# Loading C by heads from two queues at the start of a fused state-space and hardswish kernel

## Chip, cores and metric

The kernel runs on one core of one Trainium2 chip. The metric is the device time of one execution in microseconds; where several executions were timed, their median is given with the lowest and the highest.

A core has a matrix engine (PE, with its weight loads listed apart as PEld), a vector engine (DVE), a scalar engine (ACT), GpSimd (POOL) and a synchronisation engine (SP). Each has its own instruction stream and works through it in order; they wait for each other on semaphores. In this kernel DMA loads and stores are issued by SP and, for two loads at the start, by ACT.

## The reference, cut to what is computed

```python
batch, n_heads, seq, head_dim, d_state = (4, 8, 768, 32, 16)
...
for c in range(nc):                       # chunks of tokens
    cum = np.cumsum(la, axis=-1)          # la: log of the clipped a
    L = np.exp(cum[:, :, :, None] - cum[:, :, None, :]) * causal
    CB = np.einsum('bhin,bhjn->bhij', Cc, Bc)
    y_intra = np.einsum('bhij,bhjd->bhid', CB * L, xc)
    y_inter = np.einsum('bhin,bhnd->bhid', Cc, state) * np.exp(cum)[:, :, :, None]
    y[:, :, sl] = y_intra + y_inter
    Bx = np.einsum('bhjn,bhjd->bhjnd', Bc, xc) * decay_from_j[:, :, :, None, None]
    state = decay_full[:, :, None, None] * state + np.sum(Bx, axis=2)
...
x = y.transpose(0, 2, 1, 3).reshape(3072, 256)
h = x @ w_in                              # w_in: 256 x 2048
g = h * np.clip(h + 3.0, 0.0, 6.0) / 6.0
out = g @ w_out                           # w_out: 2048 x 256
```

x, a, B and C come as 32-bit floats. The two weight matrices come as 64-bit floats, which the kernel decodes into 32-bit floats itself.

## The kernel before, in words

**Tiling.** The sequence of 768 tokens is cut into six chunks of 128. A chunk has all four batches and eight heads; within a chunk the decays are kept for two halves of 64 tokens. For each chunk the state-space part gives `yT` (256 model columns by 512 tokens), and the two matrix products follow: `h`, sixteen tiles of 128 columns, and the output. Later chunks use a scheme of seven products with sums of weights in place of eight; the first chunk (0) doesn't. The loop over chunks overlaps the products of one chunk with the state-space part of the next.

**The order is written out by hand.** Tiles take their semaphores from the program, but each engine carries its instructions out in the order of the source. The opening, lines 938 to 985, is a list of calls that sets up chunk 0: everything there must be done before the first `mlp_in` (L616) can start. DMA loads take one of eight semaphores in turn, so a load that comes round to a semaphore waits, on its issuing engine, for the load that had it before.

**Names that matter.**

- `load_bc(0)` (L85) loads C and B of chunk 0. C goes through `pairs_first` (L96): eight loads on SP, one for each batch and each parity of head, of 32 KB in pieces of 256 bytes. The result `pairs` has in its partitions four pairs of heads by 32 groups of four tokens. B goes through `tokens_first` (L91): one load of 256 KB in pieces of 64 bytes, for chunk 0 on ACT's queue.
- `load_w(0)` (L142) brings the first quarter of `w_in`, 1 MB of 64-bit numbers, on ACT's queue, ahead of B. `load_x(0)` and `load_w(1)` follow on SP; `load_w(2)` and `load_w(3)` stand further down in the opening.
- `decode(i)` (L187) is a generator that turns a quarter of weights into 32-bit floats. Each `weights(i, n)` carries it on by n steps. For quarter 0 the steps are: (1) ACT copies the top words, `ws` (L198), and DVE makes the significands in two steps (L201, L205); (2) DVE picks exponent bits and sign (L215, L217); (3) ACT turns exponents into a scale (L221); (4) again on ACT (L223); (5) DVE joins them (L228, L236) into `w_in`.
- `log_a`, `add_up`, `in_three`: the logarithms, the running sums (a DVE scan, L269, in two parts) and their split into three parts, from which PE builds differences in PSUM (`diff`, L348 and L357).
- `diff_exp(c, b)` (L365): ACT takes the exponential of a difference bank. For chunk 1, batches 2 and 3, these banks are the same ones that the first chunk's state products (L539) and outputs write to.
- `first_eto` (L376): the decay from the start of the chunk.
- `turn_squares` (L465): DVE transposes `pairs` in squares of 32; `part_heads` (L472): two copies by parity of the head. Together they give C as `cT` and `csT`. `turn_b` (L431): PE transposes B (L422), ACT copies it to `bT`.
- `ends(0, b)` (L396): POOL scales B by the decays, `bs`. `fade` (L478): POOL scales half of `csT`.
- `scores(0)` (L527, L539): PE makes C times B, `cb`, and then the state products from x and `bs`. `multiply(0)`: ACT copies `adds` and `mid`, DVE multiplies the decays by `cb` (L568).
- `turn_cum` (`c_ps`, L316), `busy` (L490, two matmuls whose result nobody reads), `mix` (L594, L500), `keep` (ACT's four copies to `yT`, L608).
- `store_rows` (L286, L288) stores the running sums to DRAM, from where later chunks read their decays.

Of the kernel before, what the change touches and what calls it, by code (L numbers as in the profile page):

```python
# [8 lines left out]
FP32 = mybir.dt.float32  # L9
# [11 lines left out]
def kernel(  # L21
# [24 lines left out]
    nc = tc.nc  # L46
    P = 128
    NB, NH, S, D = x.shape
    N = B.shape[-1]
# [14 lines left out]
    loads = ctx.enter_context(tc.tile_pool(name="loads", bufs=2))  # L64
# [17 lines left out]
    Bs, bcs, xts = {}, {}, {}  # L82
    TURN = 3

    def load_bc(c):  # L85

        sl = slice(c * P, (c + 1) * P)

        def tokens_first(src, queue=nc.sync, **where):  # L91
            t = loads.tile([P, NB * NH, N], FP32, **where)
            queue.dma_start(out=t, in_=src[:, :, sl, :].rearrange("b h s n -> s (b h) n"))
            return t

        def pairs_first(src):  # L96
            t = loads.tile([P, 2, NB, 4, N], FP32, name="pairs", tag="bc")
            for b in range(NB):
                for h in range(2):
                    nc.sync.dma_start(  # L100
                        out=t[:, h, b].rearrange("s a n -> s (a n)"),
                        in_=src[b, h:NH:2, sl, :].rearrange("h (s a) n -> h s (a n)", a=4))
            return t

        if 0 < c < TURN:
            bcs[c] = [tokens_first(C, name="C", tag="bc")]
        Bs[c] = tokens_first(B, nc.scalar if c == 0 else nc.sync, name="B")
        if c == 0:
            bcs[c] = [pairs_first(C), Bs[c]]
        elif c < TURN:  # L110
            bcs[c].append(Bs[c])
        else:
            bcs[c] = [pairs_first(C), pairs_first(B)]
# [14 lines left out]
    def load_w(i, queue=nc.sync):  # L128

        raw = loads.tile([P, NK * FP * 2 * P], U32, name="raw", bufs=NRAW)  # L130
        if i < NP:
            cols = slice(2 * i * FP * P, 2 * (i + 1) * FP * P)
            src = moe_w_in[:, cols].rearrange("(k p) f -> p k f", p=P)
            dst = raw.rearrange("p (k f) -> p k f", k=NK)
        else:
            r0 = (i - NP) * FP * P
            src = moe_w_out[r0:r0 + FP * P, :].rearrange("(k p) m -> p k m", p=P)
            dst = raw.rearrange("p (k m) -> p k m", k=FP)
        queue.dma_start(out=dst, in_=src)
        raws[i] = raw  # L140

    load_w(0, nc.scalar)  # L142
    load_bc(0)
    load_x(0)
    load_w(1)
# [9 lines left out]
    def conceal_in(t, pattern):  # L155
# [24 lines left out]
        out=head, in_=head, pattern=[[-2 * N, NQ], [-N, 2]], compare_op=ALU.is_ge,  # L180
        fill=0.0, base=0, channel_multiplier=1)
    nc.gpsimd.affine_select(
        out=head, in_=head, pattern=[[2 * N, NQ], [N, 2]], compare_op=ALU.is_ge,
# [66 lines left out]
    ends_at = (slice(0, 2 * P), slice(2 * P, S))  # L250
# [17 lines left out]
    def add_up(sl):  # L268
        nc.vector.tensor_tensor_scan(  # L269
            out=cum[:, sl], data0=run.rearrange("g c p -> g (c p)")[:, sl], data1=a_sb[:, sl],  # L270
            initial=0.0, op0=ALU.mult, op1=ALU.add)
# [13 lines left out]
    def store_rows():  # L285
        nc.sync.dma_start(  # L286
            out=cum_e[1:].rearrange("c g p -> g c p"), in_=cum_c[:, 1:])
        nc.sync.dma_start(  # L288
            out=cum_d[2:].rearrange("c a g i -> g (c a) i"),
            in_=cum[:, 2 * P:].rearrange("g (k i) -> g k i", i=HT))  # L290
# [71 lines left out]
    def diff_exp(c, b):  # L362
        if c not in Ls:
            new_decays(c)
        nc.scalar.activation(Ls[c][:, b], ds.pop((c, b)), AF.Exp)  # L365

    def first_eto():

        e_ps = ps.tile([P, NB, HT], FP32, name="e_ps", tag="f0")
        for b in range(NB):  # L370
            nc.tensor.matmul(
                out=e_ps[:, b],
                lhsT=picks[:, b * P:(b + 1) * P],
                rhs=split[:, 0, HALF[1]], start=(b == 0), stop=True, skip_group_check=True)
        etos[0] = att.tile([P, NB, P], FP32, name="eto")
        nc.scalar.activation(etos[0][:, :, HALF[1]], e_ps, AF.Exp)  # L376
# [14 lines left out]
    def ends(c, b):  # L391

        if b == 0:
            bss[c] = att.tile([P, G, N], FP32, name="bs")
        hs = slice(b * NH, b * NH + NH)
        nc.gpsimd.tensor_tensor(  # L396
            out=bss[c][:, hs], in0=Bs[c][:, hs],
            in1=Ls[c][:, b, :, HT - 1:HT].to_broadcast([P, NH, N]), op=ALU.mult)
# [8 lines left out]
    def turned(c):  # L407
        if c not in bTs:
            bTs[c] = [att.tile([P, NB, P], FP32, name="bT", bufs=1),
                      att.tile([P, NB, 2, P], FP32, name="cT", bufs=1),  # L410
                      att.tile([P, NB, P], FP32, name="csT", bufs=1)]
        return bTs[c]

    def turn_ps(c, j):

        if c < 2:
            return ps.tile([P, NB, P], FP32, name="t_ps", tag=f"f{2 * j if c else 1}")
        return ps_o.tile([P, NB, P], FP32, name="t_ps", tag="o")

    def transposes(c, j, t_ps):  # L420
        for b in range(NB):
            nc.tensor.transpose(  # L422
                out=t_ps[:, b],
                in_=bcs[c][j][:, b * NH:(b + 1) * NH].rearrange("s h n -> s (h n)"),
                identity=ident)

    def turn_b(c):

        t_ps = turn_ps(c, 1)
        transposes(c, 1, t_ps)  # L430
        nc.scalar.copy(out=turned(c)[0], in_=t_ps)  # L431
# [31 lines left out]
    def turn_squares(t, out):  # L463

        nc.vector.transpose(  # L465
            out=out.rearrange("r b (s a) -> r b a s", a=4),
            in_=t.rearrange("s t b a n -> s (b a) t n"))

    def part_heads(c):
        _, cT, csT = turned(c)  # L470
        for t in range(2):
            nc.vector.tensor_scalar(  # L472
                out=cT[:, :, t], in0=csT, scalar1=parity[:, t:t + 1], scalar2=None,
                op0=ALU.mult)

    def fade(c, sl=slice(0, P), engine=nc.vector):
        csT = turned(c)[2][:, :, sl]
        engine.tensor_tensor(out=csT, in0=csT, in1=etos[c][:, :, sl], op=ALU.mult)  # L478
# [443 lines left out]
    def load(c):  # L922
        load_bc(c)
        load_x(c)
# [3 lines left out]
    def weights(i, n):  # L928
        for _ in range(n):
            next(parts[i], None)  # L930


    def diff(c, *bs):
        for part in (diff_less, diff_pick):
            for b in bs:
                part(c, b)
# [10 lines left out]
        mask_again(0, b)  # L947
    diff(0, 0, 1)
    diff(0, 2, 3)
    weights(0, 1)  # L950
    for b in range(NB):
        diff_exp(0, b)
    first_eto()
    diff(1, 2, 3)
    weights(0, 1)
    for b in range(NB):
        ends(0, b)
    turn_b(0)
    diff(1, 0, 1)
    weights(0, 1)  # L960
    diff_exp(1, 2)
    diff_exp(1, 3)
    turn_squares(bcs[0][0], turned(0)[2])
    part_heads(0)
    fade(0, HALF[1], nc.gpsimd)
    add_up(ends_at[1])
    store_rows()
    load_w(2)
    weights(0, 1)
    scores(0)  # L970
# [22 lines left out]
    for k in range(NC):  # L993
        gTs[k] = ffn.tile([P, NF, TB], FP32, name="gT")
        c, ahead = k + 1, k + 2
# [70 lines left out]
        for i, _ in enumerate((wide_units if c < NC else out_units)(k)):  # L1066
            if i == 0:
                s = NJ - 1
# [58 lines left out]
```

## Time and profile before

| What | Value |
|---|---|
| median of 3 runs | 355.81 us (355.05 to 355.95) |
| the profiled execution's own time | 355.29 us |
| its span, first to last instruction | 353.6 us |
| PE busy | 343.7 us, 97% of the span |
| DVE busy | 227.4 us, 64% |
| ACT busy | 178.7 us, 51% |
| POOL busy | 138.0 us, 39% |
| granted PE clock | 1.000 |
| read from HBM, written | 21.07 MB, 3.29 MB |

The profile is of one execution. The span leaves out 1.7 us that lie around the instructions. Times inside it are in microseconds from its start. Busy time of PE is the time in which a matmul is under way, so a high share means that PE is seldom without one. A row of the timeline gives start, length, engine, source line, operation, what is written and read, and in brackets how long the engine stood idle before and what ended that. The chain of waits is found backwards from the last instruction: at each step it goes to what released it.

The opening, in windows (us from the start, then busy time of each engine with the number of instructions, granted clock, DMA share, GB/s):

```profile
0.00:7.40 7.40, 4.42 (x10) 1.38 (x10) 4.46 (x17) 3.13 (x5) 2.75 (x13) 1.00 0.84 189
7.40:13.00 5.60, 5.35 (x144) 3.37 (x144) 2.73 (x6) 3.82 (x8) 1.52 (x4) 1.00 0.82 113
13.00:22.76 9.76, 6.58 (x294) 5.00 (x295) 9.34 (x15) 5.68 (x11) 1.50 (x1) 1.00 0.99 303
```

The engines stand in the order PE, PEld, DVE, ACT, POOL.

### The profile page before, as it was taken

The numbers are of one execution on the slowest core, as the hardware profiler recorded it, in microseconds if no ns is written. First come the engines' busy times: TensorE is split into PE (matmuls) and PEld (weight loads), VectorE is DVE, ScalarE is ACT, GpSimd is POOL, SyncE is SP. The second block draws the span as 40 slices with busy tenths as digits, with TensorE's granted clock in tenths as the row PEclk, the third lists the DMA queues.
The fourth block names the chain that finished last, engine by engine and source line by source line (L and its number), as shares of the span: only waits on it lengthen the run. The fifth ranks groups of instructions, "written<-read, shape, count | busy, mean of one in ns | idle before, by whom it ended". The sixth has DMA issues, their size and how long they took to land.

```text
span 353.6 us, 8557 instructions
## 1 busy us (share of the span) xinstructions
PE 343.7 (97%) x3488; PEld 281.9 (80%) x3488; DVE 227.4 (64%) x426; ACT 178.7 (51%) x394; POOL 138.0 (39%) x139
## 2 busy tenths in 40 slices
PE   6699999999999999999999999999999999999996
PEld 2454458888887888888888888888888888888996
DVE  6689999975797437786437787436687322688111
ACT  4768887258764741665641575551575011466100
POOL 3300000362498621099612099710078600068700
PEclk9999999999999999999999999999999999999999
DMA  8999969502925052256034256001200001200000
GB/s 168 178 335 162 272 157 122 128 2 78 164 55 66 4 125 51 35 70 81 2 72 97 36 67 91 4 4 18 34 9 1 4 3 20 34 8 2 0 32 30
DMA packets 91607, 24.92 MB, mean 70 GB/s; under 512 B 84208, under 2 KB 87952, under 8 KB 91056
## 3 DMA queue, kind: packets, MB, share of 16 engines
q1 hardware_dynamic: 87184, 23.06, 35.7%
q10 hardware_dynamic: 4384, 1.31, 1.7%
q8 instruction: 27, 0.44, 0.5%
q14 instruction: 12, 0.10, 0.1%
HBM read 21.07 MB, written 3.29 MB: 69 GB/s over the span
## 4 chain that ended last, share of the span: by engine, by line
PE 91%; DVE 3%; DMA 3%; ACT 1%; SPq 1%; issue 1%; DVEq 0%; ACTq 0%
PE even L658 18%; PE odd L658 13%; PE wb L836 12%; PE wc L836 8%; PE o L713 8%; PE h L616 8%; PE wa L836 8%; PE oa L772 4%; PE ob L772 4%; PE y L594 3%; PE y L500 2%; PE cb L527 2%; DMA raw<-in_moe_w_in_dram 2%; PE y L539 1%; DMA pairs<-in_C_dram 1%; SPq L100 1%
## 5 line engine op out<-in xcount | busy, mean ns | idle before, releaser
L758 POOL TENSOR_TENSOR s<-gT 128x512 f32<-128x512 f32 x20 | 26.3, 1317 | 86.0 <-DVE gT L699 86.0
L658 PE MATMUL even<-ts,w_sum 128*128 128x256 f32 x160 | 48.2, 383 | 0.0
L694 ACT ACTIVATE gT<-odd,half 128x512 f32<-128x512 f32 x40 | 27.5, 688 | 34.9 <-DVE odd L687 34.9
L658 PE MATMUL odd<-yT,w_in 128*128 128x256 f32 x160 | 41.1, 379 | 0.0
L673 ACT COPY even<-odd 128x512 f32<-128x512 f32 x40 | 23.0, 576 | 27.7 <-PE odd L658 25.5
L658 PEld LDWEIGHTS even<-ts,w_sum 128*128 128x128 f32 x160 | 29.9, 190 | 5.3 <-ACT up L680 1.5
L699 DVE SCALAR_TENSOR_TENSOR gT<-gT,odd 128x512 f32<-128x512 f32 x40 | 27.5, 688 | 9.9 <-ACT gT L694 9.9
L658 PEld LDWEIGHTS odd<-yT,w_in 128*128 128x128 f32 x160 | 30.4, 190 | 4.1
L385 ACT ACTIVATE L<-L,cum_n 128x64 f32<-128x64 f32 x128 | 31.5, 340 | 0.0
L836 PE MATMUL wb<-s,w_out 128*128 128x256 f32 x128 | 30.7, 382 | 0.0
L694 ACT ACTIVATE gT<-even,half 128x512 f32<-128x512 f32 x40 | 27.8, 695 | 4.4 <-PE even L658 4.4
L699 DVE SCALAR_TENSOR_TENSOR gT<-gT,even 128x512 f32<-128x512 f32 x40 | 27.2, 679 | 4.4 <-ACT gT L694 4.4
L713 PE MATMUL o<-w_out,gT 128*128 128x256 f32 x128 | 28.7, 381 | 0.0
L616 PE MATMUL h<-yT,w_in 128*128 128x512 f32 x64 | 27.7, 594 | 0.0
L674 DVE COPY up<-odd 128x256 f32<-128x256 f32 x40 | 16.9, 423 | 15.8 <-ACT even L673 15.1
L713 PEld LDWEIGHTS o<-w_out,gT 128*128 128x128 f32 x128 | 24.1, 190 | 3.7 <-issue 0.5
L403 POOL TENSOR_TENSOR tmp<-state,eto 128x256 f32<-128x256 f32 x5 | 3.4, 684 | 60.4 <-DMA eto<-cum_e 51.1
L836 PEld LDWEIGHTS wb<-s,w_out 128*128 128x128 f32 x128 | 24.0, 190 | 3.4
L758 POOL TENSOR_TENSOR s<-s,gT 128x512 f32<-128x512 f32 x20 | 25.5, 1273 | 1.6
L758 POOL TENSOR_TENSOR gT<-gT 128x512 f32<-128x512 f32 x20 | 25.4, 1272 | 0.0
L758 POOL TENSOR_TENSOR s<-gT,s 128x512 f32<-128x512 f32 x20 | 25.4, 1270 | 0.0
L658 PE MATMUL even<-yT,w_sum 128*128 128x256 f32 x80 | 24.4, 387 | 0.2
(150 smaller groups left out, 657.9 us busy)
## 6 DMA issues: line engine op xcount, KB each, us to landing
raw<-in_moe_w_out_dram SPq DMA_DIRECT2D x4, 1024.0 KB
L<-cum_d SPq DMA_DIRECT2D x8, 512.0 KB
xt<-in_x_dram SPq DMA_DIRECT2D x6, 512.0 KB
raw<-in_moe_w_in_dram SPq DMA_DIRECT2D x3, 1024.0 KB
out_dram<-back SPq DMA_DIRECT2D x128, 16.0 KB
eto<-cum_e SPq DMA_DIRECT2D x20, 64.0 KB
B<-in_B_dram SPq DMA_DIRECT2D x5, 256.0 KB
raw<-in_moe_w_in_dram ACTq DMA_DIRECT2D x1, 1024.0 KB
```

The lines of the kernel that those rows point to most:

```text
L385: nc.scalar.activation(Ls[c][:, b, h], Ls[c][:, b, h], AF.Exp, bias=cum_n[:, c, g:g + 1])
L594: nc.tensor.matmul(out=ys[c][a, u][d0:d0 + D, b], lhsT=xt[rows, b * NH + h], rhs=Ls[c][rows, b, h], start=(b == 0 and a >= min(c, 1)), sto ...
L616: nc.tensor.matmul(out=h.rearrange("p r i -> p (r i)"), lhsT=w_in[:, j, f * P:(f + 1) * P], rhs=yTs[k][:, j].rearrange("p b i -> p (b i)") ...
L658: nc.tensor.matmul(out=bank[:, r], lhsT=lhsT, rhs=rhs, start=start, stop=True, skip_group_check=True)
L673: nc.scalar.copy(out=even, in_=odd[:, 1:2].to_broadcast([P, 2, 2 * P]))
L674: nc.vector.tensor_copy(out=up[:, 1], in_=odd[:, 0])
L694: nc.scalar.activation(gTs[k][:, f], h.rearrange("p r i -> p (r i)"), AF.Relu, bias=half, scale=1.0 / 6.0)
L699: nc.vector.scalar_tensor_tensor(out=g, in0=g, scalar=1.0, in1=h.rearrange("p r i -> p (r i)"), op0=ALU.min, op1=ALU.mult)
L713: nc.tensor.matmul(out=o[:, b % 2], lhsT=gTs[0][:, f, b * P:(b + 1) * P], rhs=w_out[:, f], start=(f == 0 and b % 2 == 0), stop=True, skip_ ...
L758: nc.gpsimd.tensor_tensor(out=o, in0=p_, in1=q_, op=op)
L772: nc.tensor.matmul(out=bank[:, slot], lhsT=lhs[:, j], rhs=rhs[:, j], start=(clear and j == 0), stop=True, skip_group_check=True)
L836: nc.tensor.matmul(out=bank[:, slot], lhsT=lhs[:, j], rhs=rhs[:, j], start=(clear and j == 0), stop=True, skip_group_check=True)
```

## The change

Four things change, all in the opening.

1. C of chunk 0 is loaded by `heads_first`: eight loads, one for each head, each into 32 partitions with all four batches. The size and the pieces of 256 bytes are those of before, and so is the layout of the result. The first three go out on ACT's queue, the other five on SP's. `load_w(0)` stands on ACT's queue behind those three.
2. B of chunk 0 goes out on SP's queue behind C, ahead of x.
3. `turn_squares` and `part_heads` move up, from behind the exponentials of chunk 1 to directly behind the difference matmuls, ahead of the first step of decoding.
4. The first step of decoding moves down behind `diff_exp(0, b)` and `first_eto`; the second behind `turn_b`. The second scan and `store_rows` move up ahead of it.

```diff
+        def heads_first(src, between):
+            t = loads.tile([P, 2, NB, 4, N], FP32, name="pairs", tag="bc")
+            for i in range(NH):
+                if i == 3:
+                    between()
+                (nc.scalar if i < 3 else nc.sync).dma_start(
+                    out=t[32 * (i // 2):32 * (i // 2) + 32, i % 2].rearrange("s b a n -> s b (a n)"),
+                    in_=src[:, i, sl, :].rearrange("b (s a) n -> s b (a n)", a=4))
+            return t
...
-        Bs[c] = tokens_first(B, nc.scalar if c == 0 else nc.sync, name="B")
         if c == 0:
-            bcs[c] = [pairs_first(C), Bs[c]]
+            bcs[c] = [heads_first(C, lambda: load_w(0, nc.scalar))]
+        Bs[c] = tokens_first(B, name="B")
+        if c == 0:
+            bcs[c].append(Bs[c])
...
-    load_w(0, nc.scalar)
     load_bc(0)
...
     diff(0, 2, 3)
-    weights(0, 1)
+    turn_squares(bcs[0][0], turned(0)[2])
+    part_heads(0)
     for b in range(NB):
         diff_exp(0, b)
     first_eto()
+    weights(0, 1)
     diff(1, 2, 3)
-    weights(0, 1)
+    add_up(ends_at[1])
+    store_rows()
     for b in range(NB):
         ends(0, b)
     turn_b(0)
+    weights(0, 1)
     diff(1, 0, 1)
     weights(0, 1)
     diff_exp(1, 2)
     diff_exp(1, 3)
-    turn_squares(bcs[0][0], turned(0)[2])
-    part_heads(0)
     fade(0, HALF[1], nc.gpsimd)
-    add_up(ends_at[1])
-    store_rows()
     load_w(2)
```

## The prediction

> **What bounds the kernel now.** I read the busy table first: TensorE (PE) is busy 97% of the span. The slices place the idle rest: of the 40 only the first two and the last show 6 tenths, all others 9 or more, and a table of windows says it finely: PE is busy 16.36 of the first 22.76 us, 27.74 of the 27.74 up to 50.50, and 299.64 of the 303.10 behind that. So the opening is what can be won, and whatever moves PE's first `h` matmul (22.76) moves the end by as much. The chain of waits in order of time (start us, length us, what), for the opening:
>
> ```profile
> 0.80 5.81 DMA raw<-in_moe_w_in_dram
> ...
> 6.63 0.67 SPq L100
> ...
> 7.34 1.47 SPq L100
> ...
> 8.86 3.94 DMA pairs<-in_C_dram
> ...
> 12.97 1.10 DVE csT L465
> ...
> 14.10 0.89 DVE cT L472 x2
> ...
> 15.13 1.25 PE cb L527 x60
> ...
> 16.38 1.30 DVE L L568 x2
> ...
> 17.72 0.43 PE c_ps L316 x4
> 18.15 1.05 PE d L490 x2
> ```
>
> C is late. SP's sixth C load waits until the first weights (w0) have landed (6.62), since it reuses their semaphore; the last leaves at 8.86 and lands at 12.79. Then transpose, parity copies, scores, product, and PE's mixing until `h`. C is slow too, by the DMA totals of two windows (4 to 5.5 us, then 8 to 10 us; columns: packets, MB, packets' time as a share of 16 engines):
>
> ```profile
> q10 hardware_dynamic: 212, 0.59, 100.8%
> ```
> ```profile
> q10 hardware_dynamic: 479, 0.03, 18.6%
> q1 hardware_dynamic: 266, 0.07, 18.3%
> ```
>
> q10 is ACT's queue (w0, then B), q1 is SP's (a, C, x, w1). While w0 flows no C packet moves, though four C loads are out; later C moves 0.07 MB in 2 us with the DMA engines a third busy.
>
> **The change, part by part.**
>
> *C by heads[...].* In that window 266 C packets of 256 B take 18.3% x 16 x 2 us, 22 ns each. [...] All of C, 1024 packets, is then an estimate of [...]64 x 22 ns = 1.4 us by the row spread over 16 engines[...]. I take 1.4: the window in which x flows has more packets per engine than C needs, and only the last two pieces (0.35 us, or 0.7) stand on the path.
>
> *Order of issue.* ACT now issues three C pieces, then w0. At 0.49 us each (its B issue), w0 leaves at 2.27, not 0.80, and the table load ends at 4.1, not 3.1; `Ln` began at 4.28, so 0.2 us of cover is left there. On SP pieces four to six leave at once; the seventh waits for the first, the eighth for `a` (whose reader starts at 3.97), so all have left by 4.5. The last two arrive while w0 flows and, by the first window, wait for its end. w0's reader started at 6.64; shifted in full by 1.47 it is 8.1. But w0's start was slow: 0.95 MB of its 1.05 moved only after 2.5 us, and C's first pieces now pay for that start. So w0 is in between 6.6 and 8.1, and C lands between 7.0 and 8.5. **I take 7.45.** Its own reader on DVE isn't before 9.5, so w0 itself is covered by 1.4 us or more.
>
> *Transpose and parity copies ahead of decoding.* DVE ends the split at 7.42. The transpose began 0.18 us after the last landing (12.79 to 12.97), so now at 7.63. By the distances of starts in the timeline: to the copies 1.13, to the next 0.80, w0's two significand steps 0.73 and 1.14, the second scan 1.20. L215 (exponent bits) then runs 12.63 to 13.05. It began at 9.32: that is the price of C first, and it reaches ACT.
>
> *Exponentials ahead of the top words.* The `exp` group and `eto` end at 11.01 as before, since PE feeds them. The `ws` copy (1.10) now stands behind them, in front of `bT`, and waits for no one by then: `bT` ends at 12.6, before 12.55. PE's order is unchanged and reaches the scores at 12.85 (its diff group ends at 12.98 now, 0.16 earlier with B in time). So cb runs 12.85 to 14.1, and the product L568 14.1 to 16.6, 2.3 us earlier.
>
> *What is late next.* ACT's rows:
>
> ```profile
> 12.45 1.15 ACT L221 ACTIVATE we<-we,bias_hi 128x1024 bf16<-128x1024 uint16 x1
> 13.50 1.07 ACT L365 ACTIVATE L<-d 128x512 f32<-128x512 f32 x2
> 14.46 1.15 ACT L223 ACTIVATE we<-we,bias_lo 128x1024 uint16<-128x1024 bf16 x1
> ```
>
> The reader is to see the order: the two L365 free the banks that PE's state matmuls L539 need, and they queue behind L221, which needs L215. New: L221 at 13.06, L365 from 14.11 to 15.18, then L539 from 15.22 for 0.86, so 16.08. Before, L539 began at 16.25 right behind cb. PE idles 1.1 us there, and its waiting L539 holds up c_ps, the busy matmuls and the mixing behind it. From c_ps to mixing was 1.42 (17.72 to 19.14), from mixing to `h` 3.62. So mixing at 17.5 (L568 is done at 16.6) and **`h` at 21.15, 1.6 us earlier.**
>
> *B, x, w1 in one queue.* B goes from ACT's queue to SP's, past C, ahead of x and w1. SP's issue shows how that blocks (timeline of SP):
>
> ```profile
> 27.91 4.09 SPq L93 DMA_DIRECT2D B<-in_B_dram  x1
> 32.05 2.18 SPq L118 DMA_DIRECT2D xt<-in_x_dram  x1
> ```
>
> A small-packet load behind another holds the queue until that one has drained. B: 3280 packets in 1.5 us at 33 to 34.5, so 4096 in 1.9; from C's end (7.0 to 8.1) it is in by 9.4 to 10.5. Its readers are PE at 11.15 and POOL: covered. x took some 4.1 us in its later load (from 34.5 until w_out starts at 38.6): in by 13.9 to 15.0; L539 at 15.22: covered by 0.2 to 1.3. w1 needs another 3.0 to 4.0 (1.05 MB at 360 GB/s is 2.9): in by 17 to 18.7, before 19.1. Its `ws` copy sits in ACT's order ahead of the four yT copies. The second of these starts at 21.48 and would be at 19.9, so w1 may land as late as 18.7. cum_e, cum_d and w2 on SP follow w1's issue: before, from 16.13; now some 14, as the scan ends at 12.7.
>
> *POOL.* `bs` now runs beside DVE work. The nearest row for such company is the fade L478, 1.50 us beside DVE; the same size alone is 0.68 (tmp L403). So `bs` may take 3.3 us for 1.5: done by 11.2 to 12.8, read at 14.1 by L568. Covered.
>
> The sum: 1.6 us off the profiled execution's 355.29 (span 353.6 to 352.0) is 353.7. The median of the runs shown, 355.81, stands 0.52 above that execution, so I forecast 354.2.
>
> **Rivals.**
>
> 1. *As forecast*, C by 7.0 to 7.8: gain 1.2 to 1.9, median 353.9 to 354.6. Chance 0.56.
> 2. *C hides behind the postponed w0.* Full shift: C lands at 8.5, DVE starts at 8.68, each step slips 1.05, and the gain is 0.55: 355.3. For it: no C packet moved in w0's window. Against: the slow start. Chance 0.19.
> 3. *The other side: SP's queue becomes the bound.* B, x and w1 are in series, each blocked by the one before; w1's top-word copy stands in front of the yT copies on ACT. Price: one us per us that w1 lands after 18.7; it is a loss only after 18.7 + 1.6 = 20.3. If B drains only at 10.5, x takes 4.2 and w1 3.9, and 1.5 us are lost at each of the two blocked issues (between C and B of the next chunk the windows from 31 to 33 us show 40 and 32 GB/s, between 130 and 138), w1 lands at 21.6; `h` is then 2.9 behind 21.15, 1.3 behind 22.76: 357.1. For it: SP's w1 issue was blocked for 3.88 us already. Against: the DMA engines stood two thirds idle from 8 to 11 us, and B's packets aren't more than before. Chance 0.15.
> 4. *More than forecast.* The chain has 0.44 us of "issue" between PE's mixing matmuls at 20.09; if a shifted instruction stream loses it, and C is early, the gain is 2.2: 353.6. Chance 0.10.
>
> That the change doesn't do what it says is hardly one: the instruction order has it in place on every engine.
>
> **Numbers.** A measurement of this kernel can tell about 0.3%, 1.07 us, from no change. Case 1 is faster by more (0.54 of its 0.56), case 2 mostly within (0.15 within, 0.04 faster), case 3 mostly slower (0.13, and 0.02 within), case 4 faster: 0.68 faster, 0.19 within, 0.13 slower. The range 353.4 to 356.0 takes cases 1, 2 and most of 4, and leaves out the upper case.
>
> **What would show it.** `h` starts at 21.0 to 21.4 in the chain of waits, with ACT L365 and PE L539 in place of the DMA of C. The transpose waits little or nothing behind the split. L221 waits for DVE L215. POOL's 5.5 us wait for B shrinks to under 4. Wrong would be: a transpose after 8.5 (case 2); a wait of ACT's second `ws` copy for w1 beyond 18.7 or of PE L539 for x (case 3); `h` at 22 or later.

## The result, and the profile after

| | Before | After |
|---|---|---|
| median, both in one series | 355.62 us (355.05 to 355.95, 4 runs) | 360.94 us (359.79 to 361.24, 4 runs) |
| profiled execution, own time | 355.29 us | 359.79 us |
| its span | 353.6 us | 358.1 us |
| first `h` matmul in the chain, length of that stretch | 22.83, 27.66 us | 25.84, 29.13 us |

The changed kernel is slower: the ratio is 1.0137, 95% interval 1.0113 to 1.016 (the two medians alone give 1.015), where 354.2 us had been forecast. Executions of the kernel before differ among themselves (354.9 to 360.2 us at granted clocks from 1.00 to 0.98) by the clock that this section turns on, so its median lies between 355.6 and 356.9 from series to series; every ratio below is against the runs of its own series.

The chain of waits of the changed kernel, in order of time (start us, length us, what). Its lines stand some 11 further down than before: L476 is the transpose, L226 the exponent bits, L232 the exponent step, L376 the exponentials, L550 the state products, L501 the busy matmuls, L605 and L511 the mixing, L627 `h`.

```profile
3.30 5.63 DMA pairs<-in_C_dram
8.94 0.51 issue
9.45 1.12 DVE csT L476
...
14.78 0.50 DVE we L226
...
15.30 1.15 ACT we L232
16.45 0.98 ACT L L376 x2
...
17.52 0.85 PE y L550 x49
18.36 0.42 PE c_ps L327 x4
18.79 2.00 PE d L501 x2
20.79 1.21 PE y L605 x60
22.00 1.37 issue
23.37 0.30 PE y L605 x2
...
25.84 29.13 PE h L627 x64
```

Down to L550 this is the chain that was forecast, late by 2.3 us: C, DVE in one run up to the exponent bits, ACT's exponent step, the two exponentials, the state products. Below L550 nothing was moved by the change, yet most of the loss arises there. The 4.5 us between the spans, by the starts in the two chains ("issue" is time in which PE waited for nothing that the profile shows):

| Stretch | Before | After | Difference |
|---|---|---|---|
| to `c_ps` | 17.72 | 18.36 | +0.64 |
| busy matmuls | 1.05 | 2.00 | +0.95 |
| first part of the mixing | 0.88 | 1.21 | +0.33 |
| the "issue" pause inside it | 0.44 | 1.37 | +0.93 |
| rest up to `h` | | | +0.16 |
| `h` of the first chunk | 27.66 | 29.13 | +1.47 |

Two busy matmuls of the same shape at twice the length are PE at half rate. The windows say so: first the changed kernel, then the kernel before (columns as in the windows of the kernel before; the third number from the right is the granted clock).

```profile
18.00:22.00 4.00, 4.00 (x99) 2.10 (x92) 3.65 (x7) 2.43 (x5) 0.00 (x0) 0.57 1.05 399
...
25.00:29.00 4.00, 4.00 (x25) 2.16 (x21) 0.48 (x1) 2.94 (x4) 0.00 (x0) 0.57 1.04 310
```

```profile
18.00:22.00 4.00, 3.56 (x148) 2.44 (x147) 3.93 (x8) 1.85 (x4) 0.00 (x0) 1.00 1.03 373
...
25.00:29.00 4.00, 4.00 (x11) 1.83 (x10) 3.45 (x5) 3.36 (x5) 0.00 (x0) 1.00 0.85 300
```

By the clock records the half clock lasted from 18.52 to 21.94 and from 25.35 to 28.76, 3.41 us each. What stands in front of each is in PE's timeline (idle time before a row, and what ended it, in brackets):

```profile
17.52 0.85 PE L550 MATMUL y<-xt,bs 64*32 64x64 f32 x64 [2.83 <-ACT L L376]
...
23.37 0.30 PE L605 MATMUL y<-L,xt 64*32 64x64 f32 x2 [1.37 <-issue]
```

So PE stood still twice, for 2.83 us behind ACT and for 1.37 us for nothing that the profile names, and ran at half rate after each. It was not idle all through the 3.41 us ahead of each half clock: it was busy for 1.00 and 2.04 us of them. The order of events speaks for the idle time as the cause, but that is not shown yet.

ACT's rows show the queue of the forecast, with the wait for L226 in front:

```profile
15.30 1.15 ACT L232 ACTIVATE we<-we,bias_hi 128x1024 bf16<-128x1024 uint16 x1 [2.18 <-DVE we L226]
16.35 1.06 ACT L376 ACTIVATE L<-d 128x512 f32<-128x512 f32 x2
17.31 1.15 ACT L234 ACTIVATE we<-we,bias_lo 128x1024 uint16<-128x1024 bf16 x1
```

And C's last pieces did wait for w0. The DMA totals from 4 to 5.5 us and from 7 to 8.6 us (q10 carries what ACT issued, by then w0; q1 what SP issued; packets, MB, share of 16 engines):

```profile
q10 hardware_dynamic: 85, 0.35, 87.2%
q1 hardware_dynamic: 31, 0.01, 2.0%
```
```profile
q1 hardware_dynamic: 2279, 0.19, 145.3%
q10 hardware_dynamic: 32, 0.08, 12.3%
```

The last two C pieces were issued at 3.30 and 3.66; only when w0 was ending, near 7 to 7.5, did SP's queue move on, with B's small packets, issued at 4.13, in among C's. C landed at 8.93.

### The profile page after: what moved, and what is told of

The parts are those of the page before. It is cut to its first block, busy times and chain, and to the rows that moved or that the text cites. A ratio compares the mean times of both kernels' runs of the same rounds, so it can differ in the third digit from the quotient of the medians.

```text
span 358.1 us, 8559 instructions
## 1 busy us (share of the span) xinstructions
PE 345.9 (97%) x3488; PEld 283.1 (79%) x3488; DVE 227.9 (64%) x426; ACT 179.1 (50%) x394; POOL 139.1 (39%) x139
## 3 DMA queue, kind: packets, MB, share of 16 engines
HBM read 21.07 MB, written 3.29 MB: 68 GB/s over the span
## 4 chain that ended last, share of the span: by engine, by line
PE 90%; DVE 4%; DMA 2%; ACT 2%; issue 1%; DVEq 0%; ACTq 0%
PE even L669 18%; PE odd L669 13%; PE wb L847 12%; PE h L627 8%; PE wc L847 8%; PE o L724 8%; PE wa L847 8%; PE oa L783 4%; PE ob L783 3%; PE y L605 3%; DMA pairs<-in_C_dram 2%; PE y L511 2%; PE cb L538 1%; PE y L550 1%; PE d L501 1%
## 5 line engine op out<-in xcount | busy, mean ns | idle before, releaser
L627 PE MATMUL h<-yT,w_in 128*128 128x512 f32 x64 | 29.2, 619 | 0.0
L685 DVE COPY up<-odd 128x256 f32<-128x256 f32 x40 | 16.9, 423 | 15.8 <-ACT even L684 15.0
L407 POOL TENSOR_TENSOR bs<-B,L 128x128 f32<-128x128 f32 x24 | 13.9, 589 | 29.4 <-ACT L L396 22.1
```

The lines of the kernel that those rows point to most:

```text
L407: nc.gpsimd.tensor_tensor(out=bss[c][:, hs], in0=Bs[c][:, hs], in1=Ls[c][:, b, :, HT - 1:HT].to_broadcast([P, NH, N]), op=ALU.mult)
L627: nc.tensor.matmul(out=h.rearrange("p r i -> p (r i)"), lhsT=w_in[:, j, f * P:(f + 1) * P], rhs=yTs[k][:, j].rearrange("p b i -> p (b i)") ...
L685: nc.vector.tensor_copy(out=up[:, 1], in_=odd[:, 0])
```

## Experiments

Four questions followed: whether C behind w0, ACT's order, or the pause makes the loss; what the pause is; whether idle PE drops the clock; and whether a version with all three changed beats both kernels. Line numbers shift by one to three between the kernels.

### The two halves alone

`e1_loads_only` is the changed kernel's loads with the old order of work, `e2_order_only` the old loads with the new order (points 3 and 4 of the change).

> New loads (C by heads, first weights behind three pieces, B on SP), old order of the opening. Theory (the new order puts DVE's whole decoding behind a C that lands at 8.9 us; the loads by themselves do no harm): the first h matmul starts at about 21.2 us against 22.8 before, no stretch of half clock, time 353.5 to 355. Rival (the loads are the cost: weights 1.8 us later, B, x and second weights in one queue): h at 24 us or later, time 358 or more.

Measured: 360.55 us (358.02 to 361.0), ratio 1.0101 (1.0054 to 1.0148). A miss, and near its rival: w0 came later, ACT copied its top words at 9.53 with the exponentials queued behind, and C, in by then, was turned only at 12.37. A pause of 1.71 us in the mixing and one stretch of half clock were there too.

> Old loads, new order of the opening. Theory (the order costs whenever C is late): C lands at 12.8 us, the exponent bits on DVE come at 18 us, PE's state matmuls at 20.6, PE is idle for some 6 us and its clock halves; h at 26.5 us or later, time 360 to 363. Rival (the loads are the cost): within 1 us of before, 355 to 356.5.

Measured: 365.3 us (362.11 to 365.81), ratio 1.023 (1.0176 to 1.0284). As expected in kind, and dearer. PE's rows:

```profile
21.31 1.47 PE L539 MATMUL y<-xt,bs 64*32 64x64 f32 x64 [4.64 <-ACT L L365]
...
27.83 0.30 PE L594 MATMUL y<-L,xt 64*32 64x64 f32 x2 [1.66 <-issue]
```

DVE waits for C until 13.31, the exponent bits come at 18.67, PE idles 4.64 us for the exponentials. Two stretches of half clock of 6.8 us each. With the old loads the order is thus a loss by itself. With the new ones it is within the intervals (1.0137 with it, 1.0101 without it in `e1`).

### C in front of w0

`e4_w0_behind_c`: the changed kernel with w0 on SP's queue behind all of C.

```diff
-                if i == 3:
-                    between()
...
+            between()
             return t
...
-            bcs[c] = [heads_first(C, lambda: load_w(0, nc.scalar))]
+            bcs[c] = [heads_first(C, lambda: load_w(0))]
```

> The changed kernel with the first weights on SP's queue behind all eight pieces of C, so that no piece of C waits for them. Theory (the last two pieces of C stood behind the weights): C lands by 5.5 us, DVE's transpose starts at 7.0 right behind the split, the weights land at about 8.4 as in the changed kernel, exponent bits at 12.0, PE's state matmuls at 14.6, clock 1.00, h at 20.5 to 21 us, time 353 to 354.5. Rival (the order itself costs, whenever C lands): h above 24 us, time 358 or more.

Measured: 359.32 us (358.85 to 360.55), ratio 1.009 (1.0058 to 1.0121). The transpose starts at 6.67, right behind the split, and the state products at 15.87 after only 0.72 us of idling: the theory on C is right. The time is a miss, for `h` starts at 25.07, because the pause has grown:

```profile
15.87 0.85 PE L549 MATMUL y<-xt,bs 64*32 64x64 f32 x64 [0.72 <-DMA xt<-in_x_dram]
...
21.44 0.42 PE L604 MATMUL y<-L,xt 64*32 64x64 f32 x2 [2.43 <-issue]
```

What PE gained by starting earlier it waited in the pause, and half clock followed (20.85 to 27.68).

### The exponentials in front of the exponent step

`e3_exp_first`: the changed kernel with two lines exchanged.

```diff
     diff(1, 0, 1)
-    weights(0, 1)
     diff_exp(1, 2)
     diff_exp(1, 3)
+    weights(0, 1)
```

> The changed kernel with the two exponentials of chunk 1 moved ahead of the third decoding step on ACT, so that PE's state matmuls no longer wait for DVE's exponent bits. Theory (that wait makes PE idle for 2.8 us, and the idleness halves the clock): PE idles under 1.5 us ahead of c_ps, the granted clock stays at 1.00, the two busy matmuls take 1.05 us again, h at 22 to 22.8 us, time 354.5 to 356. Rival (late loads and slow issue cost, not this wait): L539 earlier, but h at 24.5 us or later and time 359 or more.

Measured: 356.76 us (355.16 to 359.16, 20 runs), ratio 1.0015 (0.9993 to 1.0037), slower than expected. Still, by the ratios the exchange takes back 1.2%, 4.3 us, of the 1.4%, although C is as late as in the changed kernel. The 20 executions spread with the clock: eight of 355.2 to 355.8 us had 0.995 or more, seven of 358.3 to 359.2 had 0.985 to 0.990. The profiled one is among those seven. Its state products start at 15.56 in place of 17.52, but PE waits a second time, for DVE, the half clock lasts from 17.44 to 27.68, and `h` starts at 25.03:

```profile
15.56 0.85 PE L550 MATMUL y<-xt,bs 64*32 64x64 f32 x64 [1.10 <-DMA xt<-in_x_dram]
18.04 0.63 PE L327 MATMUL c_ps<-ident,pre 32*128 32x32 f32 x4 [1.62 <-DVE L L579]
```

So the expected full clock came in some executions and not in others. What goes with it is taken up below, under "How much idle time".

### What the pause is

The pause stands in each of these kernels but `e3` in front of the last two of a group of 64 mixing matmuls, as it does in the kernel before (0.44 us); `e3`, at half clock, reaches that place only at 21.5. I numbered PE's instructions in the trace (matmuls, weight loads and the few waits between them) from 0: it is always in front of number 705. And the trace has a queue "instruction" with single packets of 16 KB, 27 in the kernel before for its 7000 PE instructions, as many as these have numbers 193, 449, 705 and so on, 256 apart. In the kernel before the first three packets start to move at 10.78, 18.12 and 24.07 us and the numbers 193, 449 and 705 start at 10.63, 16.28 and 20.52; in the changed kernel it is 10.11, 21.07 and 24.99 for the packets and 10.11, 17.54 and 23.37 for the numbers. From these six I took as an estimate that a block is asked for 256 instructions ahead, that of number 705 at number 449, just behind the start of the state products (later packets also start ahead of such a number, by up to 5.6 us). To move the boundary and not the work, 70 tiny matmuls (140 instructions on PE) were put in earlier, where PE has idle time: ahead of `turn_b` as shown, in the kernel before ahead of `scores`.

```diff
+    def tiny(n):
+        bank = ps.tile([P, NB * P], FP32, name="d", tag="f0")
+        for _ in range(n):
+            nc.tensor.matmul(
+                out=bank[HALF[0], :HT], lhsT=ident_h[:, :HT], rhs=ident_h[:, :HT],
+                start=True, stop=True, tile_position=(0, 0), skip_group_check=True)
...
+    tiny(70)
     turn_b(0)
```

> C ahead of the first weights as in e4, and 70 tiny matmuls (64 x 64, result read by nobody) in PE's wait for B. They move every later PE instruction on by 140 places, so that the block that e4 asks for at 15.9 us is asked for at about 13.9, before the second weights flow, and they keep PE busy. Theory: that block is moving by 14.5 us, no pause at the old place; a shorter one of 0 to 1.5 us may come 128 instructions before h, since the next block is asked for at 16.7; h at 20.5 to 22 us, clock 1.00 up to h, time 353.5 to 355.5. Rival (the pause belongs to the mixing matmuls or to the clock): a pause of 2 us or more at the same place, time as e4.

> The kernel before, with 70 tiny matmuls (result read by nobody) ahead of the scores, where PE is idle from 13.0 to 15.0 us. Theory (block asked for 1.5 us earlier, PE busy through the idle stretch): the pause of 0.44 us is gone, h at 22.2 to 22.5 us, no half-clock window in the opening in most runs, median 354.6 to 355.5 and the runs closer together. Rival (PE's own matmuls cost and nothing else changes): same or up to 1 us slower.

> The changed kernel with 70 tiny matmuls (result read by nobody) in PE's wait for B. Theory (of the 5.3 us, some 1 is the pause, some 2.5 the half clock that follows the idle PE, the rest the late C): the pause of 1.4 us goes, since the block is asked for at 13.5; the idle stretch ahead of the state matmuls stays and with it one half-clock window in many runs; h at 23 to 24.5 us, time 356.5 to 359. Rival (all of it is the late C): time within 0.5 us of the changed kernel.

Measured: 363.91 us (360.77 to 365.56; on top of `e4`), 366.67 (364.69 to 368.76; the kernel before), 363.59 (362.38 to 365.87; the changed kernel), with ratios 1.021 (1.0144 to 1.0276), 1.0311 (1.0243 to 1.0379) and 1.0219 (1.0168 to 1.027). All three are misses, by 5 to 11 us. The times say little, since the tiny matmuls take PE's time (2.35 us in the kernel before) and the shift brings out further stops later on. The place says it. First `e7`, then `e8`:

```profile
18.49 0.27 PE L557 MATMUL y<-xt,bs 64*32 64x64 f32 x2 [1.33 <-issue]
...
24.78 0.65 PE L612 MATMUL y<-L,xt 64*32 64x64 f32 x24 [2.51 <-issue]
```
```profile
21.30 0.30 PE L547 MATMUL y<-xt,bs 64*32 64x64 f32 x2 [2.12 <-issue]
```

The pause has left the mixing for the state products; it is again number 705, and in `e7` a second one is number 961, 256 further. It belongs to the instruction stream, not to any matmul. The 16 KB packet arrives 1.2 to 1.5 us ahead of each end: at 22.08 in the changed kernel, where PE goes on at 23.37, at 19.98 and 21.44 in `e4`, at 19.00 and 20.52 in the kernel before.

Why is it late? In `e6_pieces` each of w1, w2 and w3 is loaded in four parts, on top of `e4`, so that something may slip in between.

```diff
-        queue.dma_start(out=dst, in_=src)
+        if 0 < i < NP:
+            for k in range(NK):
+                for f in range(2):
+                    fs = slice(f * FP * P, (f + 1) * FP * P)
+                    queue.dma_start(out=dst[:, k, fs], in_=src[:, k, fs])
+        else:
+            queue.dma_start(out=dst, in_=src)
```

> C ahead of the first weights as in e4, and the second, third and fourth weights each in four loads of a quarter. Theory (PE's pause of 2.4 us in the middle of its mixing is its instruction stream: the 16 KB block is asked for when PE passes into the state matmuls at 15.9 us and waits behind 1 MB weight loads on the same DMA engines until 19.1): the block starts moving by 17.5, the pause is under 1 us, h at 21 to 22.5 us, and the time 354 to 356. If whole queues and not single loads take turns, the pause stays at 2 us or more, and so does the time of e4. Rival (the pause is the clock or something of the matmuls themselves): pause unchanged.

Measured: 358.24 us (355.49 to 359.5), ratio 1.0033 (1.0005 to 1.006). The packet moved from 18.72 on, in place of 19.10, and the pause was 1.78 us, where under 1 had been expected. A little better; it doesn't settle it.

### Holding the weights back

Here w1, w2 and w3 leave on ACT's queue among the copies of the product, from 16.9 us on in `e10`, and w1's decoding starts behind `keep`: on top of `e4` (`e10`), of the changed kernel (`e11`), of the kernel before (`e12`), and of `e4` with the old order of work (`e13`).

```diff
     load_x(0)
-    load_w(1)
...
-    load_w(2)
     weights(0, 1)
     scores(0)
     multiply(0)
-    load_w(3)
+    for i in range(1, NP):
+        load_w(i, nc.scalar)
...
-    weights(1, 1)
...
     keep(0)
-    weights(1, 3)
+    weights(1, 4)
```

> After's order and C's loads, w0 on SP's queue behind C, and the loads of w1, w2 and w3 issued on ACT's queue only after ACT's copies in the product (about 16 us), so that no weights flow while PE's next block of instructions is fetched. Theory (the pause of PE is its instruction stream standing in the DMA engines behind 1 MB weight loads): the instruction packet moves within 1 us of the start of the state products, the pause is under 0.5 us, the clock stays at 1.00, h starts at 20.5 to 21.2 and the time is 353.5 to 354.8. Rival (the pause is PE's own, whatever flows): a pause of 2 us or more stays and the time is that of the same kernel with early weight loads, about 359. A w1 that lands too late for its decoding would show as waits of DVE and ACT behind the start of h, not in front of it.

> The changed kernel with nothing altered but the loads of w1, w2 and w3, held back in the same way. Theory: the pause of 1.37 us goes, but C still lands behind w0 near 8.9 and PE still idles before the state products, so h starts near 22.3 to 23 and a stretch of half clock may stay: 356 to 358.5. Rival (the pause is not of the weight loads): as the changed kernel, 361.

> The kernel before with the same three loads held back. Theory: its issue gap of 0.44 us goes and h starts near 22.3, 355.0 to 355.6 against 355.6. Rival (the loads compete with nothing that matters before): no difference, or slower by the lateness of w1's decoding.

> As the first of these four (C early, w0 behind C, later weights held back), but with the order of work of the kernel before: decoding of w0 first, C's transpose after the exponentials. It tells what the new order is worth once the loads are right. Theory (the order matters only because C is now early): DVE waits for w0 until about 9.2, h at 21.8 to 23, 354.8 to 356.5, about 1 to 2 us behind the first of these. Rival (the order is of no use, the exponentials behind the exponent step cost what the earlier transpose brings): equal to or faster than the first.

| | Time, us | Ratio | Largest stop at an instruction boundary | Half clock, us |
|---|---|---|---|---|
| e10 | 357.49 (356.4 to 359.06) | 1.0034 (1.001 to 1.0058) | 0.33 | none |
| e11 | 359.41 (358.14 to 360.97) | 1.0083 (1.0055 to 1.0111) | none | 16.90 to 23.72 |
| e12 | 358.85 (357.0 to 359.24) | 1.0063 (1.0044 to 1.0083) | none | 15.80 to 22.63 |
| e13 | 357.8 (357.54 to 359.94) | 1.0058 (1.0036 to 1.008) | 0.36 | 12.41 to 15.83 |

On the pause all four agree with the theory. The DMA totals of `e10` from 16 to 18.1 us show the instruction block nearly alone; those of the changed kernel from 18 to 22.1 us, in which it moves from 21.07 on, show weights at 104% of 16 engines beside it:

```profile
q10 hardware_dynamic: 7, 0.03, 8.2%
q8 instruction: 1, 0.02, 2.8%
```
```profile
q1 hardware_dynamic: 841, 1.63, 103.7%
q8 instruction: 1, 0.02, 1.5%
```

But the weights are not all of the pause. Counted from the instruction 256 places ahead, PE went on 3.45 us later in `e10` and in `e13`; where PE stopped in the openings of the other kernels, with weights or x in flight, it was 3.7 to 6.3 us. And in `e7` to `e9`, where all boundaries have moved by 140, three further stops (two in `e7`) appear, each a multiple of 256 behind number 705. The longest in `e8` stands where the DMA engines have next to nothing to move (its row, and the totals from 292 to 296.5 us):

```profile
296.48 0.34 PE L508 MATMUL y<-csT,mid 32*64 32x64 f32 x7 [1.75 <-issue]
```
```profile
q8 instruction: 1, 0.02, 1.8%
```

PE had got through the 256 instructions ahead of it in 1.9 us; the block took 3.6. So a block takes some time of its own, and can stop PE where PE runs through 256 short instructions faster; weights in flight lengthen that time.

On the time all four expectations missed. `e10` started `h` at 21.69 by PE's rows, a full microsecond ahead of the kernel before (22.76), and gave it back: w1 landed near 22, DVE had nothing to decode for 3.75 us, and PE then waited for DVE, so that the output product began at 51.14 and not at 50.33. DVE's and PE's rows of `e10`:

```profile
23.29 0.43 DVE L224 TENSOR_SCALAR we<-ws 128x1024 uint16<-128x1024 uint16 x1 [3.75 <-ACT ws L207]
```
```profile
29.55 2.84 PE L625 MATMUL h<-yT,w_in 128*128 128x512 f32 x6 [0.72 <-DVE gT L708]
```

This also hides what the order of work is worth: `e13` starts `h` 1.2 us later than `e10` and is 0.3 us slower, within the intervals. In `e11` and `e12` half clock is there without any pause at an instruction boundary; PE idled 3.78 us (to 17.96) and 2.46 us (to 15.33), waiting for ACT's exponentials and for C.

### Idle time, pause and ACT's order, one at a time

Then B went back to ACT's queue on top of `e4`, so that B and x flow side by side and w1, left on SP behind x, comes early. `e17_b_act` is that alone; `e14_b_act_held` holds w2 and w3 back (second part of the cut below); `e15_b_act_held_exp` has the exchange of `e3` as well. `e16_after_held_exp` is `e11` with that exchange.

```diff
-        Bs[c] = tokens_first(B, name="B")
+        Bs[c] = tokens_first(B, nc.scalar if c == 0 else nc.sync, name="B")
...
-    load_w(2)
     weights(0, 1)
     scores(0)
     multiply(0)
-    load_w(3)
+    for i in range(2, NP):
+        load_w(i, nc.scalar)
```

> The first of these four without the holding: w2 and w3 leave on SP when w1 has left, near 15 to 16. Theory: the block of instructions comes behind w1 and beside w2, pause of 1 to 2 us, one stretch of half clock, 355.5 to 358, so 2 us or more above the one that holds them. Rival (w1 in time is all that matters): equal to it.

> The changed order and C's loads, w0 on SP's queue behind C, but B on ACT's queue as before the change, so that B and x flow side by side, w1 behind x on SP as always, and only w2 and w3 held back until the product. Theory: x lands near 13 to 14 and w1 by 16.5 to 17.5, before the block of instructions is asked for near 16; the block moves at once, no pause, clock 1.00, h at 20.5 to 21.3, and w1 is decoded in time, so the gain stays: 353.3 to 354.5. Rival (B and x together take as long as one behind the other): w1 lands near 19, the block waits for it, pause above 1.5, 357 or more.

> The same with the two exponentials of chunk 1 ahead of the exponent step on ACT. Theory (ACT's order ends last once x is in time): the state products start right behind the scores near 15.1 instead of 15.5, 0.2 to 0.5 less than without this. Rival (DVE's product ends last): equal.

> The changed kernel with w1 to w3 held back until the product and the two exponentials ahead of the exponent step. Theory (idle PE drops the clock): state products at 15.5 to 16, no idle stretch over 1.5 us, no pause, clock 1.00, busy matmuls 1.05, h at 21.8 to 22.8 against 25.24 without the exchange, 356 to 357.5 (w1 is still decoded late). Rival (the clock drops for another reason): half clock stays and the time is 358 or more.

| | Time, us | Ratio | PE idle for the exponentials | Pause | Half clock, us | `h` from, in the chain |
|---|---|---|---|---|---|---|
| e17 | 361.39 (359.8 to 361.98) | 1.0107 (1.0042 to 1.0172) | 3.28 | 1.28 | 15.28 to 22.11, 25.52 to 28.93 | 25.61 |
| e14 | 357.11 (356.0 to 360.31) | 1.0038 (1.001 to 1.0066) | 3.22 | none | 16.81 to 23.64 | 24.63 |
| e15 | 354.04 (353.48 to 357.86) | 0.9949 (0.9924 to 0.9975) | none | 1.26, 0.60 | none | 21.57 |
| e16 | 356.54 (356.18 to 359.63) | 1.0015 (0.9992 to 1.0038) | none | none | none | 21.79, by PE's rows |

Of the times only that of `e16` lies in the range named for it; that of `e15` was named against `e14`. PE still waits in `e16`, 0.87 us for x and 1.02 us for DVE.

**The pause.** `e17` and `e14` differ only in when w2 and w3 leave: 4.3 us by the medians. The intervals of the ratios just touch, but three of the four runs of `e17` are slower than all 22 of `e14`. In the profiled executions 1.0 us lies ahead of `h` and 1.7 in `h` itself (29.34 against 27.66 us), in the half clock that follows the pause.

**Idle PE.** `e14` and `e15` differ only in two lines on ACT, `e11` and `e16` likewise. Both pairs lose that idle stretch and the half clock together and gain 3.1 and 2.9 us (2.4 by the ratios for the second pair, which was timed in two series). The windows of `e14`, then of `e15`:

```profile
17.00:19.00 2.00, 2.00 (x68) 1.72 (x66) 1.59 (x3) 1.44 (x4) 0.00 (x0) 0.50 0.05 13
```
```profile
17.00:19.00 2.00, 1.67 (x64) 0.79 (x62) 1.97 (x3) 1.52 (x4) 0.00 (x0) 1.00 0.79 183
```

I had expected 0.2 to 0.5 us from the exchange in `e15`: the wait alone, without the clock.

**How much idle time.** The changes of the clock fall on a grid of 3.41 us (18.52, 21.94, 25.35 and 28.76 in the changed kernel), which lies differently in each execution (15.80 and 22.63 in `e12`). Windows of that grid with PE's busy time first: two of the kernel before, which hold its wait of 2.14 us, then one of `e12` with its wait of 2.46 us, then one of `e3` with its two waits.

```profile
10.68:14.10 3.42, 2.15 (x68) 1.52 (x61) 1.09 (x2) 2.47 (x6) 1.52 (x4) 1.00 1.28 168
14.10:17.51 3.41, 1.98 (x128) 1.68 (x128) 3.13 (x5) 1.87 (x4) 1.50 (x1) 1.00 0.84 240
```
```profile
12.39:15.80 3.41, 0.95 (x64) 0.87 (x60) 2.59 (x4) 3.10 (x5) 0.51 (x2) 1.00 0.98 103
```
```profile
14.03:17.44 3.41, 1.28 (x95) 0.91 (x79) 3.38 (x6) 1.46 (x2) 2.47 (x3) 1.00 0.92 282
```

In the kernel before the wait is cut in two by the grid, PE is busy for 63% and 58% of the two windows, and the clock stays full. In `e12` the wait lies in one window (28%), in `e3` two shorter waits add up in one (38%), and half clock follows. Over all 18 profiles, of the windows that begin in the first 33 us and ran at full clock, all 13 with PE busy for less than 48% were followed by half clock, none of the 94 above 68%, and 4 of the 11 between. So it is the idle time within one window that goes with the half clock, and not the longest wait alone; where the grid falls can decide. This is read off the traces; no run tested it.

**The three together**: `e15` beats both kernels. Its chain around the start of `h`:

```profile
13.98 0.30 PE y L549 x4
14.28 1.26 issue
15.54 0.82 PE y L549 x51
16.37 0.36 PE c_ps L326 x4
16.73 1.05 PE d L500 x2
...
21.57 10.50 PE h L626 x24
```

Scores and state products follow each other, the busy matmuls take 1.05 us again, and `h` is 1.26 us earlier than before, which is the whole gain of its span (353.6 to 352.3). It still stops for instructions, here at numbers 449 and 705. The first of these blocks moved between 12.75 and 14.25, behind the small packets of x and beside the first of w1.

## Why the prediction was wrong, step by step

- *What bounds the kernel*: right, but not all of it. Getting C early (`e4`) was not enough; the stream of PE's instructions bounded the same stretch, and showed before only as 0.44 us.
- *C by heads, 1.4 us*: the piece form is not what failed. In `e4` all of C has moved by 5.2 us, and a packet took 18 ns on average, against 22 ns in the window of the prediction. The spread over 16 engines was my estimate; on how many the pieces ran is not shown.
- *C lands at 7.45, between 7.0 and 8.5*: failed, 8.93. The step was the discount for w0's slow start. The full shift, my second rival, was right in its mechanism and still short by 0.4 us; B's packets came in among C's last pieces, which may be the rest. The transpose began at 9.45 and not 7.63.
- *From the transpose to L539*: the mechanism and its order were right, DVE up to the exponent bits, then L221, L365, L539. Forecast 7.6 us long (7.63 to 15.22), measured 8.1 (9.45 to 17.52).
- *PE idles 1.1 us there*: 2.83, and the price was wrong in kind. I counted only the wait. PE at half rate behind it cost 0.95 us in the busy matmuls and 0.33 in the first mixing.
- *"From c_ps to mixing was 1.42, from mixing to `h` 3.62"*: **this is the step that failed most.** Both distances were carried over as constants. They were 2.43 and 5.05, by half clock and by a pause of 1.37 in place of 0.44. `h` itself, counted as unchanged, took 1.47 us more. Together 3.9 of the 6.1 us between the forecast span (352.0) and the measured one (358.1); the other 2.3 are C and DVE ahead of L539, less 0.1 of rounding.
- *The covers*: `bs` took 3.66 us beside DVE (forecast 3.3) and was covered. B's readers started at 11.9, not soon after 10.5, and PE's transposes waited 1.25 us for it; POOL's wait for B grew from 5.5 to 7.3 us, where under 4 was forecast. x was in by 15.3, just beyond its range, and covered only because L550 was late.
- *Rival 3, SP's queue*: w1's top words were copied from 19.47 on, beyond the 18.7 named as the point where loss begins, but the yT copies behind stood at 22.04 for another reason, so it decided nothing here. The forecast's 360 GB/s for w1 is the mean in the kernel before from 16 to 17.5 us. Its blocked issue of B (27.91 to 32.00) ended there as the packets of the C load ahead ran out: 419 from 31 to 31.5 us, 213 and 128 in the next two half microseconds. What a late w1 costs shows in `e10`, where it landed near 22.
- *Rival 4, the 0.44 us of issue lost by a shift of the stream*: the right place to look, with the wrong sign. I saw that the gap might belong to the stream and did not ask what else the DMA engines carry when its next block is to move (weights at 104% of 16 engines in the changed kernel).
- No case on the list joined a late start of PE to the clock. The slower side was given 0.13, for a mechanism that did not act.

What stays open: why a block of instructions starts to move so late while weights flow on other queues (smaller loads in `e6` shortened its wait little; in `e15` one moved within w1's last part without a longer wait), what PE does in the 1.2 to 1.5 us between the arrival of a block and its next matmul, and what tells the windows with PE busy for 48 to 68% apart.

## What to carry to other kernels

An "issue" gap that stayed at the same instruction number while the work around it changed (number 705, in the mixing in `e4`, in the state products in `e7`) was the instruction stream here: see how long PE takes for the 256 instructions ahead of it (a block needed about 3.5 us in `e10`, with no weights in its way) and which large loads are in flight then, and let those leave a little later. Idle time of the matrix engine that gathered within 3.41 us, by one wait of 2.46 us (`e12`) or by two shorter ones (2.13 us of both in `e3`), cost its length and was followed by half the rate for 6.8 and 10.2 us, so an engine order that makes PE wait must be priced with the clock. That executions differ by where the grid falls (355.2 to 359.2 us in `e3`) is my estimate; no run tested it. And what is won at the start of a product counts only if the engine that prepares its next operands gets its own input in time (in `e10` DVE stood 3.75 us without w1, and the microsecond won was given back).

## What was not expected of the hardware

One block of 256 PE instructions, 16 KB, took 0.9 to 2.0 us to move, and where PE stood waiting for it, PE went on 1.2 to 1.5 us later; with weights in flight this held PE up for 1.3 to 2.5 us in most kernels here (0.44 in the kernel before), and in `e10` to `e14`, with later weights held back, for 0.4 us or less (in `e15`, behind x and w1, for 1.26 and 0.60). It can stop PE with idle DMA engines as well (1.75 us in `e8`). Half clock came in stretches of one, two or three times 3.41 us, after a window of that length in which PE had been busy for at most 68%. Two lines exchanged on ACT, in work that takes one microsecond, moved the kernel by 2.4 to 4.3 us.
